# Which queue loads the second weight piece and which the second token pair, in a 2:4 sparse linear layer

## The chip, the cores and the metric

One core of a Trainium2 chip. The metric is the device time of one execution in microseconds; for the kernel before, the median of 3 runs is 233.39 us (232.9 to 233.45).

## The reference

Each group of four consecutive rows of the weight keeps, in each column, the two largest by magnitude; the rest become zero. Then a linear layer with bias is computed, all in bf16:

```python
B, S, D = 16, 512, 1024            # x: (B, S, D), w: (D, D), b: (D)
wg = w.reshape(G, M, D)            # G = D // 4 groups, M = 4 rows each
mag = jnp.abs(wg)
order = jnp.argsort(mag, 1)
thr = jnp.take_along_axis(mag, order[:, M - N:M - N + 1, :], 1)   # N = 2
wp = (wg * (mag >= thr)).reshape(D, D)
return jnp.einsum("bsd,df->bsf", x, wp) + b
```

## The kernel before

The 8192 tokens are 64 tiles of 128. Every tile is multiplied by the pruned weight, which stays in SBUF: eight slices of 128 input channels, two halves of 512 output columns. A main loop (line 369) does this for tiles 14 to 63. Its tokens come transposed by DMA, and the weight lies "naturally" (wp_nat), which takes a rearranging DMA after pruning (unpack, line 172).

The first part of the kernel fills the time until those are there. The weight is loaded in pieces with four rows of a group side by side on a partition (w_gh): for the first 512 input channels (g = 0) four pieces of 256 columns, for the others (g = 1) two of 512. VectorE takes the pieces one after the other: magnitudes (abs_piece, line 120; ScalarE does the fourth piece), the second largest of four by maxima and minima (prep_piece, lines 133 to 143), the mask (150) and the pruning in place (153). TensorE meanwhile has the first eight tiles (T = 8) to multiply by each piece as it is pruned. For that it needs their first 512 channels transposed. These are loaded as they are (load_x, line 79, tiles xh), transposed on TensorE against an identity (line 182, four matmuls of 128 columns a tile), and copied from PSUM by ScalarE (line 187). The products with the pieces are at line 203; a piece gives matmuls of 256 columns.

The order of all this is written out by hand in the string FRONT, whose tokens are issued one by one, and every instruction is kept in program order on its engine. Its first tokens matter here: D.0 is a transposing DMA for tiles 8 to 13 (line 259), A and P are the magnitudes and the pruning of a piece, W and w are dummy matmuls on constants (line 105: nine of 512 columns, then short ones of 128), T.n transposes tile n, C.n copies it out, N and M are products of a piece with a tile:

```python
I.1.0.512 D.0 A.0 P.0 W W W W W W W W W w w T.0 T.1 C.0 T.2 T.3 C.1 w T.4 C.2 N.0.0.0 N.0.0.1 T.5
N.0.1.0 N.0.1.1 N.0.0.2 N.0.0.3 N.0.1.2 N.0.1.3 M.0.2 A.1 C.3 P.1 ...
```

The loads ahead of it, in lines 83 to 91, are issued on two queues: SyncE's (SP, the default) and ScalarE's (ACT, given as nc.scalar). SP has half of the first weight piece, token tiles 0 and 1 (the first pair), tile 4, tile 5, the second weight piece, the pair 6-7, and the third and fourth weight pieces together. ACT has the other half of the first weight piece and the second pair, tiles 2 and 3. Each pair is 256 KB in runs of 1 KB, each single tile 128 KB, the second weight piece 256 KB in runs of 512 B. In the trace, profile queue q1 is SP's and q10 is ACT's.

Each DMA raises a semaphore when it has landed. There are eight for these loads, used in turn, so a later DMA on SP waits for the landing of the earlier load that had its semaphore. In the trace, the DMA of line 259 waits for the load that ACT issued second.

Of the kernel before, what the change touches and what calls it, by code (L numbers as in the profile page):

```python
# [10 lines left out]
def kernel(  # L11
# [7 lines left out]
    nc = tc.nc  # L19
# [49 lines left out]
    def load_w(g, c0, c1, eng=nc.sync, m0=0, m1=4):  # L69
        dst = w_gh[(g, c0 // FH)][:, m0:m1, c0 % FH:c0 % FH + c1 - c0]  # L70
        K(eng.dma_start(dst, wv[:, g, m0:m1, c0:c1]))
# [4 lines left out]
    def load_x(ta, tb, eng=nc.sync):  # L76
        xt = const.tile([P, tb - ta, KH], bf16, name=f"xh_{ta}")
        src = xf[ta * P:tb * P, 0:KH].rearrange("(t p) c -> p t c", p=P)
        K(eng.dma_start(xt[:], src))
        for t in range(ta, tb):  # L80
            xh[t] = xt[:, t - ta, :]
# [1 line left out]
    load_w(0, 0, 256, nc.sync, 0, 2)  # L83
    load_w(0, 0, 256, nc.scalar, 2, 4)
    load_x(0, 2)
    load_x(2, 4, nc.scalar)
    load_x(4, 5)
    load_x(5, 6)
    load_w(0, 256, 512)
    load_x(6, 8)  # L90
    load_w(0, 512, 1024)
    bias_sb = const.tile([P, Dout], bf16, name="bias_sb")
# [311 lines left out]
```

## Time and profile before

| what | value |
|---|---|
| median of 3 runs | 233.39 us (232.9, 233.39, 233.45) |
| the profiled execution | 232.85 us |
| its span, from first to last instruction | 231.1 us |
| TensorE (PE) busy in the span | 226.7 us |
| VectorE (DVE) busy | 120.2 us |
| ScalarE (ACT) busy | 18.0 us |
| DMA, mean over the span | 165 GB/s |

Times in the views are microseconds from the start of the span. A row of the timeline gives start, duration, engine, line, operation and what it writes and reads; equal neighbours are merged with their number behind an x. ACTq and SPq are instructions that issue a DMA: their duration is that of the issuing. When the data are there is told by the DMA's landing. PEld is the loading of a matmul's stationary operand; for a transpose that operand is the token tile, so it is the load that waits for the tile's DMA.

### The profile page before, as it was taken

Reading aid. Unit: us, or ns where it says so; the run is one execution under the profiler, and the core shown is the slowest. Engines: PE = TensorE matmul, PEld = TensorE weight load, DVE = VectorE, ACT = ScalarE, POOL = GpSimd, SP = SyncE. Lnnn points to the kernel's source line nnn. Section 1 sums busy time; section 2 is a strip of 40 time slices with the busy share of each in tenths; the row PEclk is TensorE's granted clock in tenths of the full one; section 3 lists DMA queues with packets and bytes.
Section 4 is the critical chain, followed back from the end, with each engine's and each line's share of the span. In section 5 each row is a group of like instructions: output and inputs, shape, how many; then the busy total and the mean of one; then the engine's idle time right before and its main releaser. Section 6 shows DMA issues by size and latency. Waiting matters only on the chain.

```text
span 231.1 us, 2772 instructions
## 1 busy us (share of the span) xinstructions
PE 226.7 (98%) x1137; PEld 111.1 (48%) x1156; DVE 120.2 (52%) x213; ACT 18.0 (8%) x33; POOL 0.7 (0%) x6
## 2 busy tenths in 40 slices
PE   8999999999999999999999999999999999999995
PEld 4887444444444444444444444444444444444443
DVE  4999787867987424424424424424423423433434
ACT  3868400000000000000000000000000000000000
POOL 1000000000000000000000000000000000000000
PEclk9999999999999999999999999999999999999999
DMA  6989989999447222991249522696128950122222
GB/s 214 299 180 262 210 195 197 289 247 318 185 182 272 91 84 80 272 249 59 80 115 278 152 95 91 129 245 194 70 91 197 241 197 34 60 91 91 91 94 91
DMA packets 77228, 38.19 MB, mean 165 GB/s; under 512 B 63136, under 2 KB 69024, under 8 KB 77216
## 3 DMA queue, kind: packets, MB, share of 16 engines
q1 hardware_dynamic: 67568, 20.88, 41.4%
q10 hardware_dynamic: 9648, 17.14, 20.1%
q8 instruction: 9, 0.15, 0.3%
q14 instruction: 3, 0.02, 0.0%
HBM read 3.41 MB, written 16.78 MB: 87 GB/s over the span
## 4 chain that ended last, share of the span: by engine, by line
PE 98%; DVE 0%; issue 0%
PE bank L369 73%; PE bank L203 16%; PE bank L263 6%; PE bank L105 2%; PE bank L182 1%; DVE o_last L354 0%
## 5 line engine op out<-in xcount | busy, mean ns | idle before, releaser
L369 PE MATMUL bank<-wp_nat,xTb 128*128 128x512 bf16 x737 | 161.7, 379 | 0.8
L248 DVE TENSOR_TENSOR o_pair<-bank,bias_sb 128x512 bf16<-128x512 f32 x104 | 67.3, 687 | 99.5 <-PE bank L369 94.1
L369 PEld LDWEIGHTS <-xTb 128*128 128x128 bf16 x752 | 73.6, 98 | 88.7
L239 DVE TENSOR_TENSOR stage<-bank,stage 128x512 f32<-128x512 f32 x22 | 14.2, 687 | 4.3 <-PE bank L203 4.2
L203 PE MATMUL bank<-w,xT 128*128 128x256 bf16 x128 | 14.5, 273 | 0.0
L243 DVE TENSOR_TENSOR o_pair<-stage,bias_sb 128x512 bf16<-128x512 f32 x22 | 14.0, 684 | 0.0
L203 PE MATMUL bank<-wp_nat,xg 128*128 128x512 bf16 x62 | 13.9, 379 | 0.1
L203 PEld LDWEIGHTS <-xT 128*128 128x128 bf16 x128 | 12.3, 98 | 1.6
L235 ACT COPY stage<-bank 128x512 f32<-128x512 f32 x22 | 11.5, 613 | 4.5 <-PE bank L203 4.5
L203 PE MATMUL bank<-wp_nat,xfill 128*128 128x512 bf16 x47 | 10.6, 379 | 0.1
L263 PE MATMUL bank<-wp_nat,xfill 128*128 128x512 bf16 x47 | 10.5, 379 | 0.1
L203 PEld LDWEIGHTS <-xg 128*128 128x128 bf16 x64 | 6.3, 98 | 7.6
L263 PEld LDWEIGHTS <-xfill 128*128 128x128 bf16 x48 | 4.7, 98 | 5.7
L203 PEld LDWEIGHTS <-xfill 128*128 128x128 bf16 x48 | 4.7, 98 | 5.5
L369 PE MATMUL bank<-wp_nat,xTs 128*128 128x512 bf16 x32 | 7.1, 379 | 0.0
L150 DVE TENSOR_TENSOR mask<-mag,thr 128x512 bf16<-128x512 bf16 (+3 forms) x10 | 5.6, 584 | 0.2
L153 DVE TENSOR_TENSOR w<-w,mask 128x512 bf16<-128x512 bf16 (+3 forms) x10 | 5.6, 582 | 0.1
L105 PE MATMUL bank<-const-bfloat16-1.0 128*128 128x512 bf16 (+1 forms) x12 | 4.4, 540 | 0.8 <-PEq L388 0.8
L369 PEld LDWEIGHTS <-xTs 128*128 128x128 bf16 x32 | 3.1, 98 | 3.8
L187 ACT COPY xT<-bank 128x512 bf16<-128x512 bf16 x8 | 4.1, 605 | 2.7 <-PE bank L182 2.7
L120 DVE TENSOR_SCALAR mag<-w 128x512 uint16<-128x512 uint16 (+2 forms) x6 | 2.7, 466 | 2.5 <-DMA w<-in_w_dram 2.5
L263 PE MATMUL bank<-wp_nat,xTb 128*128 128x64 bf16 (+3 forms) x40 | 3.7, 251 | 0.0
(20 smaller groups left out, 27.1 us busy)
## 6 DMA issues: line engine op xcount, KB each, us to landing
out_dram<-o_pair ACTq DMA_DIRECT2D x25, 512.0 KB, 2.8
out_dram<-o_pair ACTq DMA_DIRECT2D x13, 256.0 KB, 2.1
wp_nat<-w SPq DMA_DIRECT2D x16, 128.0 KB, 2.9
w<-in_w_dram SPq DMA_DIRECT2D x3, 512.0 KB, 5.5
xh<-in_x_dram SPq DMA_DIRECT2D x2, 256.0 KB, 4.1
xh<-in_x_dram ACTq DMA_DIRECT2D x1, 256.0 KB, 3.8
xh<-in_x_dram SPq DMA_DIRECT2D x2, 128.0 KB, 3.6
w<-in_w_dram SPq DMA_DIRECT2D x1, 256.0 KB, 4.0
```

The lines of the kernel that those rows point to most:

```text
L105: K(nc.tensor.matmul(bank[7][:, :n], lhsT=ones[:, :P], rhs=ones[:, :n], start=True, stop=True))
L120: K(nc.vector.tensor_single_scalar(mag[:, ms].bitcast(u16), w_of(i)[:, ms].bitcast(u16), 0x7FFF, op=Alu.bitwise_and))
L150: K(nc.vector.tensor_tensor(mask[:, ms, c], mag[:, ms, c], tb, op=Alu.is_ge))
L153: K(nc.vector.tensor_tensor(w_of(i)[:, ms, c], w_of(i)[:, ms, c], mask[:, ms, c], op=Alu.mult))
L187: K(nc.scalar.copy(xt[:], src))
L203: K(nc.tensor.matmul(dst, lhsT=lhs, rhs=rhs, start=c0 == 0 and m == 0, stop=c1 == FH and m == 3))
L235: K(nc.scalar.copy(stage[(h, t)][:], bank[own[(h, t)]][:]))
L239: K(nc.vector.tensor_tensor(st, bank[own[(2 + h, t)]][:], st, op=Alu.add))
L243: K(nc.vector.tensor_tensor(get_o(t)[:, f], stage.pop((h, t))[:], bias_sb[:, f], op=Alu.add))
L248: K(nc.vector.tensor_tensor(get_o(t)[:, f], bank[bk][:], bias_sb[:, f], op=Alu.add))
L263: K(nc.tensor.matmul(bank[bk][:, :c1 - c0], lhsT=xN[t][:, kt, :], rhs=wp_nat[h][:, kt, c0:c1], start=kt == 0, stop=kt == KT - 1))
L369: K(nc.tensor.matmul(bank[bks[h]][:], lhsT=xN[t][:, kt, :], rhs=wp_nat[h][:, kt, :], start=kt == 0, stop=kt == KT - 1))
```

## The change

In the list of loads, the second weight piece (input group 0, columns 256 to 511) is issued by ScalarE's queue, where the second token pair was; the second token pair is issued by SyncE's queue, directly behind the first pair. The sizes, the destinations and all other instructions are as before.

```diff
     load_w(0, 0, 256, nc.sync, 0, 2)
     load_w(0, 0, 256, nc.scalar, 2, 4)
     load_x(0, 2)
-    load_x(2, 4, nc.scalar)
+    load_w(0, 256, 512, nc.scalar)
+    load_x(2, 4)
     load_x(4, 5)
     load_x(5, 6)
-    load_w(0, 256, 512)
     load_x(6, 8)
     load_w(0, 512, 1024)
```

## The prediction

> **What bounds the kernel now.** I read the page first (shares by engine, chain that ended last), then the timeline of the first 10 us, the DMA issues with their landings, and the waits.
>
> ```profile
> PE 226.7 (98%) x1137; PEld 111.1 (48%) x1156; DVE 120.2 (52%) x213; ACT 18.0 (8%) x33; POOL 0.7 (0%) x6
> ...
> PE 98%; DVE 0%; issue 0%
> PE bank L369 73%; PE bank L203 16%; PE bank L263 6%; PE bank L105 2%; PE bank L182 1%; DVE o_last L354 0%
> ```
>
> The chain is PE from the first dummy matmul (line 105) to the last product. There is no wait in it: what PE does is the time. So the change can take nothing away from PE; it can only put a wait into it, or not. The timeline of the start shows where (start, duration, then the instruction):
>
> ```profile
> 0.77 4.21 PE L105 MATMUL bank<-const-bfloat16-1.0 128*128 128x512 bf16 x11 [0.77 <-PEq L388]
> ...
> 1.25 0.52 ACTq L79 DMA_DIRECT2D xh<-in_x_dram  x1
> 1.25 1.43 SPq L79 DMA_DIRECT2D xh<-in_x_dram  x3
> ...
> 2.73 0.68 SPq L71 DMA_DIRECT2D w<-in_w_dram  x1
> ...
> 4.78 1.48 PE L182 MATMUL bank<-ident,xh 128*128 128x128 bf16 x16
> ...
> 6.16 0.39 PE L182 MATMUL bank<-ident,xh 128*128 128x128 bf16 x4
> ...
> 6.60 0.39 PE L182 MATMUL bank<-ident,xh 128*128 128x128 bf16 x4
> ```
>
> The 16 transposes from 4.78 are those of tiles 0 and 1 (first pair), then 2 and 3 (second pair); at 6.16 come those of tile 4, at 6.60 those of tile 5. Up to 5.63 they are 107 ns apart, soon after 56: PE's clock steps up at 5.67. The ninth, the first of the second pair, starts at 5.63. The loads that they need were issued as the rows of ACTq and SPq show, and landed after (us from issue, from the DMA issues of short stretches; in order: second pair on ACT, first pair on SP, tile 5, second weight piece, last pair 6-7):
>
> ```profile
> xh<-in_x_dram ACTq DMA_DIRECT2D x1, 256.0 KB, 3.8
> xh<-in_x_dram SPq DMA_DIRECT2D x1, 256.0 KB, 3.4
> ...
> xh<-in_x_dram SPq DMA_DIRECT2D x1, 128.0 KB, 3.6
> ...
> w<-in_w_dram SPq DMA_DIRECT2D x1, 256.0 KB, 4.0
> ...
> xh<-in_x_dram SPq DMA_DIRECT2D x1, 256.0 KB, 4.7
> ```
>
> By the trace's landing marks: first pair 4.67, second pair 5.05, tile 4 5.42, tile 5 5.82, weight piece 6.71, pair 6-7 8.16. After a landing the weight load of a transpose starts 0.04 later and its matmul 0.107 (first pair: 4.674, 4.716, 4.781). So the margins of PE now are: first pair 0.00, second pair 5.63 - 5.05 - 0.11 = 0.47, tile 4 6.16 - 5.42 - 0.11 = 0.63, tile 5 6.60 - 5.82 - 0.11 = 0.67, pair 6-7 8.57 - 8.16 - 0.11 = 0.30.
>
> **The change part by part.** No instruction is added or removed; two DMAs change places.
>
> *The weight piece, earlier.* It lands now at 6.71, and its reader is VectorE's abs of the second piece:
>
> ```profile
> DVE mag L120 <- DMA w<-in_w_dram: 2.5, 1, 2.5
> ...
> 6.86 0.42 DVE L120 TENSOR_SCALAR mag<-w 128x1024 uint16<-128x1024 uint16 x1
> ```
>
> VectorE waits for a weight DMA once only, for the first piece. It reaches the second at 6.86, right behind its last pruning of the first (6.52, 0.43 long). Landing 1.5 us sooner (in the place of the second pair, about 5.2) gains nothing: VectorE is busy without a hole from 3.35, and the product that needs this piece starts at 10.57, 0.6 after its pruning. Gain: 0. It only adds room to a margin of 0.15.
>
> *ScalarE's queue.* Issuing the piece took SP 0.68, the pair took ACT 0.52. So ACT's table load and first copy move by 0.16, to end at 3.45; its next work is the copy at 5.45. Cost: 0, covered by 2.0 us.
>
> *SyncE's queue.* The pair goes in ahead of tile 4, tile 5 and pair 6-7, each issued about 0.5 later, but still some 2 us before its turn on the wire; behind the missing weight piece the queue is 0.2 ahead. The big transposing DMA (line 259, issued 5.38) waits on the semaphore that ACT's load raises, now the weight piece's; if that lands between 5.2 and 5.9, it goes out up to 0.5 later. Its data (landed 15.25) are first read at 21.05: 0, covered by 5.8.
>
> *The second pair, later.* This is what costs. Total bytes do not change and the wire is full (328 to 373 GB/s in each half microsecond from 2.5 to 6.0), so landings only trade places. Afterwards SP carries, in order, half the first weight piece, first pair, second pair, tile 4, tile 5; ACT the other half and the weight piece. When tile 5 has landed, just those bytes have moved that had moved when the weight piece landed before: 6.71. Tile 5 took 0.40 after tile 4 and tile 4 0.375 after what was ahead, so tile 4 lands at 6.31 and the second pair at 5.93. Against the slots on PE:
> - second pair: 5.93 + 0.11 = 6.04 for 5.63: 0.41 late
> - tile 4: 6.42 for 6.16: 0.26
> - tile 5: 6.82 for 6.60: 0.22
>
> These do not add; a wait for the earlier one moves the slots of the later ones. If the weight piece is all sent before the second pair is through, PE slips 0.41; if part of it still shares the wire, the second pair comes sooner, and tile 5 alone holds PE for 0.22, since its landing depends on the sum of bytes only. Bounds: 0 (the pair in its old slot, margin 0.47 used up exactly) and 0.97 (below, a lagging engine). I take **0.3**, between 0.22 and 0.41, the rows nearest. Pair 6-7 has the same bytes ahead of it as before, lands at 8.16, and its slot has moved back as well: 0.
>
> The row on sharing: between 3.4 and 4.0, with both queues sending 1 KB packets, SP's moved 111 and ACT's 98. The Trainium skill ("DMA: Bandwidth & Descriptors", section "Queues, rings and completion order") has each DMA engine take turns between queues, packet by packet. The trace agrees roughly. By that rule, with packets of 512 B (27 ns) against 1 KB (46 ns), the weight piece gets 27/73 of the time beside the first pair, is not through when the second pair starts, and the second pair lands at an estimated 5.7; the sum by it would be 0.22, and without it up to 0.41.
>
> Nothing later gives it back: PE has no wait to absorb it.
>
> **Sum.** Profiled execution: 231.1 span + 1.75 around it = 232.85; with 0.3, 233.15. That execution was 0.54 below the median of the runs, 233.39, so I put the change on the median: **233.7**.
>
> **Rivals.**
> 1. *Nothing moves* (233.4). The second pair lands by 5.52. For: its margin is 0.47, and 1 KB packets may get more than an even share. Against: it needs the wire to carry 0.4 us of bytes less ahead of it, and tile 5 with the same bytes is late as well.
> 2. *Slower: one DMA engine lags.* A load counts as landed when the last of 16 engines is done. For pair 6-7, 15 marks came by 7.41 and the last at 8.16, 0.75 behind. Before, the pair's and tiles' margins of 0.47 to 0.67 took most of such a lag; afterwards they are gone. With it tile 5 lands at 7.46 and its matmul starts at 7.57 for 6.60: 0.97, so 234.4. It decides from a lag of about 0.5 on tile 4 or 5, or on the second pair. Against: the marks of the other loads lie within 0.4 of each other.
> 3. *The clock steps up later.* The wait falls around 5.67, where PE goes from 107 to 56 ns a transpose. Should a wait of 0.4 hold that off for as long again as the slow stretch lasted (4.9 us from 0.77), half of it is lost, 2.45: 235.8. Against: PE would still have been busy for 4.9 us before. The Trainium skill ("TensorE: Matmul & The Clock Gate", section "Part 1: The HAM clock gate") counts in free-running windows of about 3.4 us, by which the estimate would be 1.7 instead; no row here shows a second window.
> 4. *Faster by a little.* The first pair now has margin 0, and the timed runs are up to 0.6 above the profiled one: there the first transpose may wait. Beside 512 B packets the first pair should land sooner, by 0.6 at most (its packets were spread over 1.35 us, alone they are 256 x 46 ns / 16 = 0.74). If that wait goes and the second pair is in time: 232.9. Against: both must hold, and the profile shows no such wait.
>
> **How the numbers follow.** Forecast 0.50 (233.6 to 233.9, with the spread of runs 233.1 to 234.1); nothing moves 0.15; lag 0.25 (234.0 to 234.7); clock 0.03; faster by a little 0.07. A measurement of this kernel tells about 0.3%, 0.7 us, from no change: runs of before differ by 0.55. So slower (above 234.1) is the clock, most of the lag and the forecast's upper edge: 0.30. Faster (below 232.7) is half of the fourth rival: 0.04. Same: 0.66. Range 233.0 to 234.6: it leaves out the clock, part of the fourth rival and the end of the lag.
>
> **What would show it.** Afterwards the ninth transpose should start near 6.0, with an idle stretch of PE of 0.2 to 0.4 ahead of it or ahead of tile 4's or tile 5's; the weight piece should land near 5.2, tile 5 near 6.7; VectorE's abs should still start at 6.86; the first pair at or before 4.67. It is wrong if a hole over 0.7 appears, if the 56 ns pace begins later than about 6, if the second pair lands by 5.5, or if VectorE's 6.86 moves: then the weight piece did matter.

## The result, and the profile after

The changed kernel is slower: 235.03 us (median of 7 runs, 234.1 to 236.39) against 232.99 (7 runs, 232.84 to 233.45) for the kernel before; ratio 1.0084, 95% interval 1.0062 to 1.0106. Measured again beside other kernels it was 235.65 (4 runs, 234.73 to 235.99) against 233.06; ratio 1.0102, interval 1.0073 to 1.0132. The loss is 2.0 to 2.6 us, the forecast was 0.3.

The profiled execution took 235.83, with a span of 234.0 (before: 232.85 and 231.1). From its page, TensorE's share and the chain that ended last:

```profile
PE 228.8 (98%) x1156; PEld 111.7 (48%) x1156; DVE 120.2 (51%) x213; ACT 18.2 (8%) x33; POOL 0.7 (0%) x6
...
PE 96%; DMA 2%; DVE 0%; SPq 0%; issue 0%
```

A DMA now stands in a chain that was PE from end to end. TensorE's waits by cause (us in total, times, longest), and its timeline at the start (rows between are left out at the dots):

```profile
PE bank L182 <- DMA xh<-in_x_dram: 1.9, 2, 1.2
```

```profile
0.77 3.63 PE L105 MATMUL bank<-const-bfloat16-1.0 128*128 128x512 bf16 x11 [0.77 <-PEq L388]
5.11 0.64 PE L182 MATMUL bank<-ident,xh 128*128 128x128 bf16 x8 [0.71 <-DMA xh<-in_x_dram]
6.95 1.00 PE L182 MATMUL bank<-ident,xh 128*128 128x128 bf16 x8 [1.20 <-DMA xh<-in_x_dram]
...
7.85 0.63 PE L182 MATMUL bank<-ident,xh 128*128 128x128 bf16 x4
...
11.98 2.26 PE L203 MATMUL bank<-w,xT 128*128 128x256 bf16 x19
```

The row of 16 transposes is torn in two: PE waits 0.71 for the first pair and 1.20 for the second. The second pair's transposes begin at 6.95, where they began at 5.63: 1.32 late (less than the two waits, since the clock stepped up at 3.65 here and at 5.67 before, so that the dummies ended sooner). The products after tile 7 begin at 11.98, where they began at 9.02: 2.96 late, and so it stays to the end (span +2.9). The other 1.64 is pace: eight transposes took 0.64 at 5.11, but 1.00 at 6.95. The clock's records in the trace show why: full from 3.65, half from 7.06, full again from 10.47. Busy time of each engine and granted clock (the third number from the end; where the trace has no clock record, as ahead of 3.65, it reads 1.00 whatever the pace) in those two stretches:

```profile
3.65:7.06 3.41, 1.50 (x15) 0.90 (x14) 3.38 (x17) 1.07 (x2) 0.00 (x0) 1.00 0.96 310
7.06:10.47 3.41, 3.41 (x26) 2.91 (x26) 3.31 (x12) 2.15 (x4) 0.00 (x0) 0.50 1.18 346
```

PE (the first busy time) worked only 1.50 of the 3.41 us before the clock fell; then 3.41 us at half pace cost 1.7.

The landings, from the DMA issues (KB, us from issue to landing; issued at 1.26 and 1.75):

```profile
w<-in_w_dram ACTq DMA_DIRECT2D x1, 256.0 KB, 5.1
xh<-in_x_dram SPq DMA_DIRECT2D x1, 256.0 KB, 5.2
```

By the landing marks (16 to a load; the last counts): first pair 5.07 (before 4.67), weight piece 6.34, second pair 6.90 (before 5.05), tile 4 7.27, tile 5 7.61. And the wire, that is what the DMA engines move, by stretches, before and after (the last two numbers are the mean busy share of the 16 DMA engines and GB/s):

```profile
3.50:4.00 0.50, 0.50 (x2) 0.15 (x1) 0.50 (x4) 0.00 (x0) 0.00 (x0) 1.00 1.04 346
4.00:4.50 0.50, 0.50 (x2) 0.15 (x1) 0.50 (x3) 0.00 (x0) 0.00 (x0) 1.00 1.12 373
```

```profile
3.50:4.00 0.50, 0.50 (x3) 0.19 (x2) 0.44 (x3) 0.00 (x0) 0.00 (x0) 1.00 0.75 219
4.00:4.50 0.50, 0.40 (x4) 0.10 (x2) 0.50 (x4) 0.00 (x0) 0.00 (x0) 1.00 0.78 217
```

This is the find of the comparison. The prediction shared out a full wire; for one microsecond the wire was a quarter empty, though the weight piece had been issued 2.2 us and the second pair 1.7 us before.

### The profile page after: what moved, and what is told of

Read it like the earlier page. It is cut to its first block, busy times and chain, and to the rows that moved or that the text cites. A ratio compares the mean times of both kernels' runs of the same rounds, so it can differ in the third digit from the quotient of the medians.

```text
span 234.0 us, 2791 instructions
## 1 busy us (share of the span) xinstructions
PE 228.8 (98%) x1156; PEld 111.7 (48%) x1156; DVE 120.2 (51%) x213; ACT 18.2 (8%) x33; POOL 0.7 (0%) x6
## 3 DMA queue, kind: packets, MB, share of 16 engines
HBM read 3.41 MB, written 16.78 MB: 86 GB/s over the span
## 4 chain that ended last, share of the span: by engine, by line
PE 96%; DMA 2%; DVE 0%; SPq 0%; issue 0%
PE bank L369 72%; PE bank L203 17%; PE bank L263 6%; DMA xh<-in_x_dram 2%; PE bank L182 1%; DVE o_last L354 0%; SPq L79 0%; SPq L71 0%; PE bank L105 0%
## 5 line engine op out<-in xcount | busy, mean ns | idle before, releaser
L203 PE MATMUL bank<-w,xT 128*128 128x256 bf16 x128 | 15.4, 282 | 0.0
L203 PEld LDWEIGHTS <-xT 128*128 128x128 bf16 x128 | 12.8, 102 | 1.9
L182 PE MATMUL bank<-ident,xh 128*128 128x128 bf16 x32 | 3.4, 264 | 1.9 <-DMA xh<-in_x_dram 1.9
L105 PE MATMUL bank<-const-bfloat16-1.0 128*128 128x512 bf16 (+1 forms) x12 | 3.9, 485 | 0.8 <-PEq L388 0.8
```

Source lines behind the costliest of these rows:

```text
L105: K(nc.tensor.matmul(bank[7][:, :n], lhsT=ones[:, :P], rhs=ones[:, :n], start=True, stop=True))
L182: K(nc.tensor.transpose(dst[:, m, :], xv[:, m, :], ident[:]))
L203: K(nc.tensor.matmul(dst, lhsT=lhs, rhs=rhs, start=c0 == 0 and m == 0, stop=c1 == FH and m == 3))
```

## The experiments

Three theories stood at the start. *Supply*: something ahead of the wire hands out a load's packets too late, at a cost for each run (a contiguous piece, one packet). *Bytes*: only what was sent ahead counts, as predicted. *Two queues*: the loss comes from packets of unequal length on two queues at once. All kernels compute the whole reference. Diffs are against the kernel before unless said otherwise.

### The pair's half of the change

```diff
     load_x(0, 2)
-    load_x(2, 4, nc.scalar)
+    load_x(2, 4)
     load_x(4, 5)
     load_x(5, 6)
     load_w(0, 256, 512)
```

> The pair's half of the change alone: tiles 2 and 3 on SyncE's queue behind the first pair, the second weight piece back in its old place behind tile 5. All theories agree that the second pair is then in time (landing near 5.1, slot 5.63) and the time is that of before, 233.0 +- 0.3. If it is slower by 1 us or more, the pair's move to SyncE's queue is the cause by itself and all three theories are wrong.

Measured 234.1 against 233.1, ratio 1.0052 (1.0028 to 1.0076). The weight piece isn't moved here, and half of the loss is there. By the words of the expectation all three theories were wrong as they stood. The second pair landed at 6.11: 11 of the 16 engines' marks came by 4.95, the other five between 5.66 and 6.11. Its timeline on PE:

```profile
6.16 0.67 PE L182 MATMUL bank<-ident,xh 128*128 128x128 bf16 x8 [0.32 <-DMA xh<-in_x_dram]
...
9.82 0.64 PE L182 MATMUL bank<-ident,xh 128*128 128x128 bf16 x8 [0.53 <-DMA xh<-in_x_dram]
10.30 3.90 PE L203 MATMUL bank<-w,xT 128*128 128x256 bf16 x34
```

PE waits for the second pair and once more for the pair 6-7. So not all of the 1.0 is the second pair's: its transposes begin 0.53 late (6.16 for 5.63), the products after tile 7 are 1.28 late (10.30 for 9.02), and the difference comes with the pair 6-7, for which PE does not wait in the changed kernel. The Trainium skill ("DMA: Bandwidth & Descriptors", section "Issuing engines are not separate DMA queues") says that issuing from several engines "will only save the time on the sequencer it takes to initiate the DMA". That time is 0.45 for a pair on SP here; the measurement decides otherwise, since the same pair issued 0.5 later on the other queue landed about 1 us later.

The same kernel a second time:

> The pair's move alone, a second look at its landings. If the first look stands: second pair at 5.8 or later, with several of the 16 marks 0.7 or more behind the others, time 233.8 to 234.6. If it lands by 5.3 with close marks, the first look was chance.

Second pair at 5.90, five of the marks by 5.13, eleven from 5.36 on; time 235.23 for this one execution, above the expected range, because the pair 6-7 landed at 10.86 and PE waited 1.58 for it. The late pair stands; how many of the engines are late changes.

### The weight piece's half

```diff
     load_x(2, 4, nc.scalar)
+    load_w(0, 256, 512, nc.scalar)
     load_x(4, 5)
     load_x(5, 6)
-    load_w(0, 256, 512)
```

> The weight piece's half alone: it goes to ScalarE's queue, but behind the second pair, which stays there; it is issued at about 1.77, just when SyncE issues tile 4. Supply theory (packets of both queues are made one DMA after another in the order of issue, and the 512 short runs of the piece take longer to make than the wire needs for them): tiles 4 and 5 land at 6.5 or later, the wire is below 85% busy for some half microsecond after 4.5, and the time is 0.7 to 1.5 us over before. Bytes theory (only what was sent ahead counts, the wire stays full): tile 4 lands by 6.3, tile 5 by 6.7, time +0.2 to 0.3. Two-queue theory (loss from packets of unequal length on two queues at a time): like supply, but the loss begins when the second pair is through, and SyncE's tile 4 moves slowly beside the piece.

Measured 233.36 against 233.1, ratio 1.0019 (1.0008 to 1.0031). Second pair 5.30, tile 4 6.07, tile 5 6.81: tile 4 and the time are as the bytes theory has them, tile 5 is 0.1 later, and the time is about the term that the prediction had worked out. The wire had a dip here as well (0.80 busy and 238 GB/s from 3.5 to 4.0), but a short one. With the pair left on ScalarE's queue, the weight piece beside the tiles costs 0.3 and no more.

### Long runs in the weight piece's place

```diff
     load_x(0, 2)
-    load_x(2, 4, nc.scalar)
+    load_x(6, 8, nc.scalar)
+    load_x(2, 4)
     load_x(4, 5)
     load_x(5, 6)
     load_w(0, 256, 512)
-    load_x(6, 8)
```

> As the changed kernel, but in the place of the weight piece ScalarE's queue loads the token pair 6-7: the same 256 KB at the same time, in 256 runs of 1 KB instead of 512 of 512 B; the weight piece comes behind tile 5 on SyncE's queue. Supply theory: the wire stays over 95% busy from 2.5 to 6, the first pair lands by 4.8, the second pair between 5.6 and 5.95, time +0.2 to +0.5 over before. Bytes theory: the same, second pair 5.93. Two-queue theory with unequal lengths: no loss either. If the second pair lands at 6.5 or later, what counts is being second on SyncE's queue beside any DMA of 256 KB on the other, not the short runs.

Measured 233.94, ratio 1.0064 (1.0035 to 1.0094); in the profiled execution (235.59) the second pair landed at 6.73. So short runs beside it are not needed for the loss.

### One queue

```diff
     load_x(0, 2)
-    load_x(2, 4, nc.scalar)
+    load_w(0, 256, 512)
+    load_x(2, 4)
     load_x(4, 5)
     load_x(5, 6)
-    load_w(0, 256, 512)
```

> The order of the changed kernel on one queue: first pair, weight piece, second pair, tiles 4 and 5, all on SyncE's. Supply theory: the same starvation, wire below 85% busy between 3.5 and 4.5, second pair at 6.5 or later, time +1 to +3 over before. Two-queue theory: no starvation, second pair near 5.9, time +0.3 to +0.6. Bytes theory: second pair 5.93, the same +0.3 to +0.6.

Measured 234.35, ratio 1.0078 (1.0048 to 1.0109); second pair at 6.96, the 16 engines 0.52 busy from 3.5 to 4.0, at 151 GB/s. The loss does not need two queues. Of the three theories that leaves supply, on a queue by itself.

Beside what the bytes ahead of it give, the second pair is late by much the same in all these kernels. The bytes give 5.93 in the last two and in the changed kernel; measured were 6.73, 6.96 and 6.90. With the pair's move alone they give 5.1, since just the bytes are ahead that were ahead before, when it landed at 5.05; measured were 6.11 and 5.90. So the pair's lateness in the changed kernel is a sum of two terms: the bytes, as predicted, and another 0.8 to 1.0 us that the prediction did not have.

### The pairs swapped on SyncE's queue

```diff
     load_w(0, 0, 256, nc.scalar, 2, 4)
-    load_x(0, 2)
-    load_x(2, 4, nc.scalar)
+    load_x(2, 4)
+    load_x(0, 2)
```

> As the run with the pair's move alone, but the two pairs change places on SyncE's queue: tiles 2 and 3 second, tiles 0 and 1 third. That run had its third load landing at 6.1 (11 of 16 marks by 4.95, five between 5.7 and 6.1), though the bytes ahead would have let it land by 5.1. Queue theory (the third load on a queue gets its packets late, whatever it carries): tiles 2 and 3 land near 4.2, tiles 0 and 1 near 6, some of their first packets take 0.5 us or more. Address theory (it is the tokens of tiles 2 and 3 that come slowly behind those of 0 and 1): the second load has the long packets, and both land late, the second at 5 or later. Since the first transposes wait for the third load now, the time is over before by 1 to 1.5.

Tiles 2 and 3 landed at 4.69 (15 marks by 4.19), tiles 0 and 1 at 6.02; six packets of the third load took 0.9 to 1.0 us, where 46 ns is usual. Whichever pair is third is late; the addresses are not the cause. (233.74 in one execution, 0.8 over before, a little less than expected.)

### Fewer runs ahead

The two first loads bring the same 128 KB in half as many runs, as two rows of each group over 512 columns. What is left of the first two pieces comes in the second piece's old place:

```diff
-    load_w(0, 0, 256, nc.sync, 0, 2)
-    load_w(0, 0, 256, nc.scalar, 2, 4)
+    load_w(0, 0, 512, nc.sync, 0, 1)
+    load_w(0, 0, 512, nc.scalar, 1, 2)
     load_x(0, 2)
-    load_x(2, 4, nc.scalar)
+    load_x(2, 4)
     load_x(4, 5)
     load_x(5, 6)
-    load_w(0, 256, 512)
+    load_w(0, 0, 512, nc.sync, 2, 4)
```

> As the run with the pair's move alone, with the same bytes at the same places, but the two first loads bring their 128 KB in 128 runs of 1 KB instead of 256 of 512 B: rows 0 and 1 of each group over 512 columns. The rest of the first two weight pieces follows in one load of 256 KB in the second piece's place, so VectorE starts only near 7 and the time, over before by 2 or more, is of no use; what counts is the landing of the second pair. Supply by runs (packets are made at some 260 a microsecond after the issue, and 256 runs fewer are ahead): the second pair lands by 5.4, no packet over 0.5 us in it. Supply by place (third on its queue, however few runs ahead): again about 6.

> The pair's move with the two first loads in 128 runs each instead of 256, a second look. If the first look stands: second pair by 5.3, wire at least 90% busy from 3 to 5.5. If it lands at 5.7 or later, fewer runs ahead do not help and the first look was chance.

The second pair landed at 5.05 and 5.18: in time again, with the same bytes at the same places. No 1 KB packet up to 6.0 took over 0.43 us, and in the second execution the wire was 0.87 busy or more from 3.0 to 5.5, a little under what was expected. (237.5 and 237.7 in one execution each, with VectorE late as expected.) Next, fewer runs on SyncE's queue only (ScalarE's first load as before):

```diff
-    load_w(0, 0, 256, nc.sync, 0, 2)
+    load_w(0, 0, 512, nc.sync, 0, 1)
     load_w(0, 0, 256, nc.scalar, 2, 4)
     load_x(0, 2)
-    load_x(2, 4, nc.scalar)
+    load_x(2, 4)
     load_x(4, 5)
     load_x(5, 6)
-    load_w(0, 256, 512)
+    load_w(0, 0, 512, nc.sync, 1, 2)
+    load_w(0, 256, 512, nc.sync, 2, 4)
```

> The pair's move, with fewer runs ahead on SyncE's queue only: its first load brings 128 KB in 128 runs of 1 KB, ScalarE's stays at 256 of 512 B; the rest of the first two weight pieces comes behind tile 5, so the time is of no use. Supply of each queue by itself: second pair by 5.3 as with fewer runs on both. Shared supply: between, 5.4 to 5.9. If it is at 6 again, what helped before was the other queue's load.

5.28: in time as well (one execution, 237.72). Fewer and longer runs ahead on the same queue are enough. The microsecond from 3.75, in the run with the pair's move alone, with fewer runs on both queues and on SyncE's only (one line each):

```profile
3.75:4.75 1.00, 1.00 (x5) 0.45 (x4) 1.00 (x6) 0.00 (x0) 0.00 (x0) 1.00 1.03 257
```

```profile
3.75:4.75 1.00, 1.00 (x5) 0.45 (x4) 0.23 (x1) 0.00 (x0) 0.00 (x0) 1.00 1.06 331
```

```profile
3.75:4.75 1.00, 1.00 (x5) 0.45 (x4) 0.00 (x0) 0.00 (x0) 0.00 (x0) 1.00 1.06 355
```

257 GB/s against 331 and 355. In the first the engines count as busy, but with packets of up to 1.06 us that stand and wait.

One more thing differs between these lines: VectorE (the third busy time) works all through the first and hardly or not at all in the others, since its weights come later there. For these three kernels that rival is not ruled out. But VectorE's work alone does not empty the wire: in the kernel before it is as busy from 3.5 to 4.5, with 346 and 373 GB/s. Nor is it needed for a dip: in the changed order with fewer runs, below, the wire fell to 209 GB/s from 3.0 to 3.5 with VectorE busy for 0.05 us.

How many packets the queues had sent by 5.0 (packets, MB, share of 16 engines from 1.5 to 5.0; a run is a packet, but 51 to 81 packets of each kernel are not runs but the landing marks, of 4 bytes), before, in the changed kernel, with the pair's move, and with fewer runs ahead on both:

```profile
q1 hardware_dynamic: 746, 0.58, 54.6%
q10 hardware_dynamic: 544, 0.39, 33.9%
```

```profile
q1 hardware_dynamic: 590, 0.44, 42.9%
q10 hardware_dynamic: 697, 0.35, 34.7%
```

```profile
q1 hardware_dynamic: 935, 0.77, 76.1%
q10 hardware_dynamic: 272, 0.13, 12.6%
```

```profile
q1 hardware_dynamic: 878, 0.84, 78.2%
q10 hardware_dynamic: 144, 0.13, 10.8%
```

Both queues together had sent 1290 packets before the change and 1287 in the changed kernel, there with 0.79 MB for 0.97, since more of them are short. SyncE's queue came to 776 to 935 in the seven runs of the pair's move and its variants so far and the next one. It came to 1074 with the weight piece on it too, and only to 590 in the changed kernel, beside the weight piece on ScalarE's. So one rate for a queue does not describe them all.

Nor is it the number sent that makes the pair so late. The pair ends with the queue's run 768 in the first layout and with its run 640 in the others. In the four runs of the first layout run 768 started at 4.60 to 5.11, in the three of the others run 640 at 4.41 to 4.55 (marks not counted). Some 0.5 from the last packet to the landing (2.84 to 3.32 for SyncE's first load before) makes 5.1 to 5.6 and 4.9 to 5.05, an estimate. Measured were 5.9 to 6.1 and 5.05 to 5.28, in the same order. The rest of the lateness lies in how uneven the engines are: with the pair's move 11 of the 16 marks had come by 4.95.

### The pair as two loads

```diff
     load_x(0, 2)
-    load_x(2, 4, nc.scalar)
+    load_x(2, 3)
+    load_x(3, 4)
```

> The pair's move alone, but the second pair comes as two loads of one tile each, 128 runs each; the runs ahead are as before. Supply theory (runs or place on the queue): tile 3 lands at 5.8 or later as the pair did. Shape theory (a load of two tiles, whose packets go over two blocks of tokens, starts slowly): tile 2 by 4.9, tile 3 by 5.3, and the time is within 0.4 of before.

Tile 2 landed at 5.62, tile 3 at 5.94. The load's shape isn't the cause. (233.88 in one execution; with the clock full from 3.46 on it was 0.3 over the one execution of before beside it, which says little.)

### Useless short runs on either queue

Added to the pair's move, 512 runs of 64 B into a tile that nothing reads, ahead of the second pair, first on ScalarE's queue and then on SyncE's:

```diff
+    scrap = const.tile([P, 4, 32], bf16, name="scrap")
...
     load_x(0, 2)
-    load_x(2, 4, nc.scalar)
+    K(nc.scalar.dma_start(scrap[:], wv[:, 0, :, 0:32]))
+    load_x(2, 4)
```

> The run with the pair's move alone, plus a load that nothing reads on ScalarE's queue, where the changed kernel has the weight piece: 512 runs of 64 B, 32 KB in all. Bytes theory: 0.1 us later than that run. Supply shared by both queues: the second pair lands 0.6 to 1.3 later than the 6.1 of that run, near 7, as in the changed kernel. Supply of each queue by itself: near 6.1 to 6.3.

> The same useless load on SyncE's queue, between the two pairs. Bytes theory: second pair 0.1 later than without it, 6.2. Supply, shared or of each queue by itself: 0.8 to 1.8 later, 6.9 to 7.9. Beside the run with the load on ScalarE's queue it tells whether the two queues share what supplies the packets.

On ScalarE's queue: second pair at 6.04, no later than without. On SyncE's: 6.59, 0.5 to 0.7 later. So runs on the other queue did not hold the pair up, and runs on its own did (one execution each, 233.93 and 235.62, the latter with the clock at half up to 10.09). But 0.5 to 0.7 for 512 runs is not the expected 0.8 to 1.8: the short runs themselves went out quickly (about 270 packets in the quarter microsecond from 3.75). A cost for each run that is the same whatever its length is ruled out: 128 runs fewer of another length made the pair 0.6 to 1.1 sooner, 512 more of 64 B only 0.5 to 0.7 later.

### Both pairs first

```diff
-    load_w(0, 0, 256, nc.sync, 0, 2)
+    load_w(0, 0, 256, nc.scalar, 0, 2)
     load_w(0, 0, 256, nc.scalar, 2, 4)
     load_x(0, 2)
-    load_x(2, 4, nc.scalar)
+    load_x(2, 4)
```

> Both halves of the first weight piece on ScalarE's queue, one behind the other; SyncE's begins with the two pairs, the weight piece is back in its old place. The second pair is then second on its queue, with 256 runs ahead instead of 512. Queue theory in either form: it lands by 5.1, in time, and tile 4 (third on the queue now) is the late one, 5.4 to 6.2. VectorE starts 0.2 to 0.6 later, as the second half lands later, and the product of the first piece's second half (margin 0.1 before) waits for it: time +0.2 to +0.8 over before. If the second pair still lands at 5.8 or later, neither the place on the queue nor the runs ahead of it are the cause.

Measured 235.84, ratio 1.0122 (1.0087 to 1.0158), far more than expected: the first piece's halves landed at 4.50 and 5.74, so VectorE was late and PE waited 1.86 for it at 8.4, with a half stretch of the clock behind. The second pair landed at 5.55, between the two answers, all 16 marks within 0.5. There is no lag of single engines here, but the wire was slow to fill (0.6 busy around 2.75). This run decides nothing on supply.

### The changed order with fewer runs

```diff
-    load_w(0, 0, 256, nc.sync, 0, 2)
-    load_w(0, 0, 256, nc.scalar, 2, 4)
+    load_w(0, 0, 512, nc.sync, 0, 1)
+    load_w(0, 0, 512, nc.scalar, 1, 2)
     load_x(0, 2)
-    load_x(2, 4, nc.scalar)
+    load_w(0, 0, 512, nc.scalar, 2, 4)
+    load_x(2, 4)
     load_x(4, 5)
     load_x(5, 6)
-    load_w(0, 256, 512)
```

> The changed order with the same bytes in fewer runs: the two first loads are 128 runs of 1 KB (rows 0 and 1 of each group over 512 columns), the load on ScalarE's queue in the piece's place is 256 runs of 1 KB (rows 2 and 3). 768 runs come to the end of the second pair instead of 1280. VectorE starts only when that load is there, so the time is over before by 1 us or more and not to be compared; the landings are. Supply theory (a run costs the queues time whatever its length): wire at least 95% busy from 3 to 6, second pair between 5.6 and 6.0, the bytes' 5.93. If it lands at 6.5 or later, the number of runs is not the cause.

Second pair at 6.28: 0.6 sooner than in the changed kernel, not the 5.93 of the bytes, and between the two answers of the expectation. The wire still dipped, earlier (209 GB/s from 3.0 to 3.5, 195 from 3.5 to 4.0), and the first pair landed at 5.12, though only 128 runs are ahead of it on its queue. So fewer runs take back more than half of the pair's lateness over the bytes, not all of it, and the runs ahead on the same queue do not explain every late load. Measured 234.84, ratio 1.0077 (1.0062 to 1.0092), a time that holds VectorE's later start.

### The changed kernel again, and with the holes filled

> The changed kernel once more, beside the next three, for a second profile and more times. Waits alone (no half stretch of the clock) should give 234.0 to 234.7, with a half stretch 1.7 more, 235.7 to 236.4. In the profile the second pair lands at 6.5 to 7.0 again and the wire is below 85% busy somewhere between 3.5 and 4.5.

Measured as told above; second pair at 6.88, wire at 118 GB/s from 3.5 to 4.0, holes (waits of PE) of 0.96 and 1.00, half clock from 6.89 to 10.30. The four runs were 234.73 and 235.53, and with a mean clock of 0.993 235.77 and 235.99. Then the changed kernel with dummy matmuls in place of the holes:

```diff
-        I.1.0.512 D.0 A.0 P.0 W W W W W W W W W w w T.0 T.1 C.0 T.2 ...
+        I.1.0.512 D.0 A.0 P.0 W W W W W W W W W w w W T.0 T.1 C.0 W W W W W T.2 ...
```

> The changed kernel with dummy matmuls where TensorE waits: one of 512 columns ahead of the first transpose, five between the first and the second pair's. The landings stay as they are. In the changed kernel's profile the granted clock was full from 3.65 to 7.06, half from 7.06 to 10.47, and full after. Clock theory (the holes of 1.9 us cause the half stretch, which costs 1.7): no run has a half stretch behind the first dummies, the runs above 235.6 are gone, and the median is 234.1 to 234.8. If the half stretch comes all the same, or the median stays at 235 or above, the holes are not its cause.

Measured 234.35 (4 runs, 234.04 to 234.72), ratio 1.0055 (1.0038 to 1.0072). The second pair still lands late (6.71), and its transposes begin even later:

```profile
5.20 1.06 PE L182 MATMUL bank<-ident,xh 128*128 128x128 bf16 x8
6.06 1.61 PE L105 MATMUL bank<-const-bfloat16-1.0 128*128 128x512 bf16 x5
7.51 0.61 PE L182 MATMUL bank<-ident,xh 128*128 128x128 bf16 x8
```

7.51 instead of 6.95, yet this execution is 1.1 shorter than the changed kernel's profiled one: eight transposes take 0.61 there. None of the four runs shows a half stretch (3.41 us at half clock) in its mean clock, and none was longer than this one. That agrees with the holes as the cause, but does not show it alone: with 4 runs out of 11 falling without the dummies, none out of four comes by chance about one time in four. And the clock stepped up late here: the five dummies from 6.06 start 427 ns apart at first and 220 apart from 6.85. The better evidence is the stretch ahead of each fall, with PE busy for 1.50 and 1.48 of 3.41 us. How much of the median is the clock's is not sharp (1.0084 and 1.0102 against 1.0055, with intervals that touch or overlap), some 0.7 to 1.3 us. The version with dummies is still 1.4 slower than the kernel before.

## Why the prediction was wrong, step by step

- *What bounds the kernel*: right. PE had no wait, and the 2.96 by which the products after tile 7 were late reached the end (span +2.9).
- *The weight piece, earlier*: gain 0, right. But it landed at 6.34, not near 5.2. VectorE's abs of it began at 7.06, behind its own work, which had moved by 0.2 with the first piece's landing.
- *ScalarE's queue*: 0, right; its first copy ended at 3.40.
- *SyncE's queue*: 0, right. The transposing DMA was issued at 6.36, not by 5.9, as it waited for the weight piece; its data landed at 13.98, long before 21.05.
- *The second pair, later*: this is the step that failed, at "the wire is full ... so landings only trade places". The direction and the place were right; 0.3 was 1.32 in the profile. The sum of bytes gave 5.93 for the landing and 6.90 was measured, with the wire a quarter empty from 3.5 to 4.5; the 5.7 from taking turns packet by packet was further off. The full wire of before needed both queues. Packets of the two queues before the change, from 4.0 to 4.5 and from 4.5 to 5.0:

```profile
q10 hardware_dynamic: 143, 0.14, 78.1%
q1 hardware_dynamic: 57, 0.05, 34.0%
```

```profile
q1 hardware_dynamic: 167, 0.15, 91.5%
q10 hardware_dynamic: 19, 0.01, 7.7%
```

ScalarE's queue sent the second pair just when SyncE's queue sent little, though tile 4 had been issued on it 2.2 us before. The pair's half alone costs 1.0, part of it at the pair 6-7, the weight piece's half alone 0.26. Together they cost more than their sum, at least in part because the pair's margin of 0.47 covers lateness only once. The row of the pair 6-7, with one mark 0.75 behind the others, may have been a sign of it (this is not shown); I read it as one engine's lag.
- *The first pair*: forecast at or before 4.67, landed at 5.07 and 5.24 in the two profiles of the changed kernel and at 4.29 in the one with dummies. Not forecast, and not explained: the loads are the same in all three.
- *Sum*: it was put on 233.39, the median of three runs; seven runs of the kernel before gave 232.99. So the forecast of 233.7 missed the 235.03 by 1.3, but the change of 0.3 missed by 1.7.
- *Rivals 1 and 4*: neither came. The second pair landed at 6.90, not by 5.52, and the first pair came 0.4 later than before, not sooner.
- *Rival 2, one engine lags*: its price of 0.97 was nearer to the 1.32 than the forecast was, but its mechanism was too small: with the pair's move five of the 16 marks lag by 0.7 or more behind the other eleven, not one.
- *Rival 3, the clock*: I gave it 0.03. It came about in another form, a fall after an early step up, in 4 of 11 runs of the changed kernel by their mean clock (or more: an execution without clock records reads 1.000, as the profiled one with dummies does). Its price was 1.64 in the profile, about half of the 3.41 between the clock's steps, not the 2.45 from the length of the slow start. The prediction's other estimate of 1.7, from the window that the Trainium skill ("TensorE: Matmul & The Clock Gate", section "Part 1: The HAM clock gate") gives, was near. In the profile with long runs the step up itself came late, at 10.12, which is the form that I had named.

What stays open: why a queue hands out the runs of a load late that was issued long before, whether they are made late or fetched late; why some of the 16 engines wait and others do not; whether the number or the length of the runs ahead counts; and what VectorE's work has to do with it. A fixed cost for each run is excluded by the 64 B runs, an address effect by the swapped pairs, the load's shape by the split pair, the last two in one execution each.

## What to carry to other kernels

A transfer that lands in time may owe that to its queue: before moving it behind others, look at what its new queue has to send ahead of it and in what runs, and don't take the wire for full because it was full with two queues at work. Where TensorE has no margin at the start, price a wait twice: by its length, and by the stretch at half clock that a hole can bring. If such a hole can't be closed, dummy matmuls in it may be worth more than an earlier start; here the median was 0.7 to 1.3 lower with them, which the intervals hardly separate.

## What the runs showed of the hardware that was not expected

- With the token loads all on one queue, that queue sent 776 to 935 packets by 5.0 us, and 1074 with the second weight piece on it too; two queues together sent 1290. Single packets of 1 KB stood for up to 1.06 us beside a usual 46 ns.
- The clock's steps in the changed kernel lie 3.41 us apart (3.65, 7.06, 10.47). The Trainium skill ("TensorE: Matmul & The Clock Gate", section "Part 1: The HAM clock gate") has a window of that length; the trace agrees. It gives the fall to half after an idle window. Here the clock fell after stretches in which PE was busy for 1.50 and 1.48 of 3.41 us, and in four runs of other kernels after 0.77 to 1.52. It stayed full after one with 2.23 (everything on one queue), and did not step up after one with 2.54 (long runs) that ended at 6.71, only at 10.12.
